# Weight words without GpSimd, a deferred sigmoid and separate summary products in a fused attention and channel-mix kernel

## The chip, the cores and the metric

The kernel runs on one NeuronCore of a Trainium2 chip. The metric is the device time of one execution in microseconds (us). The core has five instruction streams: PE (TensorE, matrix products), DVE (VectorE), ACT (ScalarE), POOL (GpSimd) and SP (which here only issues DMA transfers). Each works through its own queue strictly in order and waits on semaphores for the others. PE has a second row in the profile, PEld, for the loads of its stationary operand.

## The reference

Two stages, one after the other. The first is attention over 4 batches, 8 heads, 768 tokens and 64 features. A query sees the keys less than 16 positions away, and besides these 24 summary keys (the maximum over each block of 32 keys) with summary values (the mean over the block):

```python
k_sum = k.reshape(B, H, nb, block, D).max(axis=3)
v_sum = v.reshape(B, H, nb, block, D).mean(axis=3)
scores_l = where(|i - j| < 16, scale * q @ k.T, -1e9)
scores_s = scale * q @ k_sum.T + log(32)
a = softmax over [scores_l, scores_s]
x = a @ [v, v_sum]                     # heads side by side: 512 features
```

The second is a channel mix on these 512 features, with each token and the one before it (`xp`):

```python
xk = mu_k * x + (1 - mu_k) * xp
xr = mu_r * x + (1 - mu_r) * xp
k  = relu(xk @ w_k) ** 2               # 512 -> 1024
v  = k @ w_v                           # 1024 -> 512
out = sigmoid(xr @ w_r) * v
```

The three weight matrices come as 64-bit floats. The kernel gets them as pairs of 32-bit words and makes the fp32 values itself.

## The kernel before, in words

**Units.** Attention is cut into 32 units: a batch, a pair of heads, a half of the 768 tokens (384, six windows of 64 queries). For one unit PE makes the scores (L480), DVE adds the mask and finds the maximum (L491), ACT takes the exponentials and their sums (L495), DVE the reciprocals (L502), POOL multiplies by them in six instructions (L506, "the norms"), PE transposes (L513), ACT copies the result out of PSUM (L517), and PE multiplies by the values (L535). In each window 96 rows are local keys and 24 are summaries. In batch 0 the block means come from PE (L416, L436), and DVE or POOL copies them six times side by side into the 24 summary rows of each value tile (L444). In the later batches a DMA does that.

**Channel mix.** For each half batch ("token tile" of 384) the shift and mix is made per pair of heads: ACT or POOL multiplies by `1 - mu` (L560 or L563), DVE adds `mu * x` (L566), ACT rounds to fp32r (L569) and DVE takes the rest (L571). With these high and low parts PE makes the gate (`w_r`, L612 to L614), whose sigmoid ACT takes (L628). Then for j = 0 to 7 the experts: twelve products with block j of `w_k` (L644), relu and square on ACT (L649, L651), a rounded part (L653 on DVE or L654 on ACT) and a rest (L655), and nine products with block j of `w_v` (L666, the last block L692), which accumulate in three PSUM banks. L698 multiplies by the gate, and a DMA stores.

PSUM has four banks named `mm`. While the experts run, three of them hold the accumulators. The fourth is passed between the products with `w_k` and the gate of the second half of batch 0, which is made in three pieces between blocks 5, 6 and 7 of the first half: the next product can start only when ACT has read the bank.

**Weights.** 20 blocks of 128 x 512 values (four `w_r`, eight `w_k`, eight `w_v`) are made while batch 0 runs. For one block: a DMA into a buffer `st` (three of them), a scaling of the high word on ACT (L323) or POOL (L326), the sign on POOL (L331, high word times zero), two instructions on DVE that shift and join the bits (L335, L339), the rounding to fp32r on ACT (L347) or POOL (L349), and the rest on DVE (L361). Buffers: two `we` for sign and low bits, two `wc` for the words that are being made.

**Order.** All of this is recorded as operations with due times. A planner then simulates the engines with a table of lengths and puts the operations in order on each engine; where an operation has two ways (ACT or POOL, DVE or ACT) it also chooses the engine. `NUDGE` shifts single due times. Warm-up products (L727) fill PE where it waits during the first 33 us. The order is fixed in the program: an engine doesn't pass over an instruction that waits.

## Time and profile before

| | |
|---|---|
| three timed runs | 471.42, 472.8, 473.5 us; median 472.8 us |
| the profiled execution | 474.23 us, of which 472.4 us lie between its first and last instruction (the span) |
| PE busy | 442.6 us, 94% of the span |
| PEld busy | 374.6 us, 79% |
| ACT busy | 293.4 us, 62% |
| DVE busy | 272.5 us, 58% |
| POOL busy | 145.6 us, 31% |
| DMA | 51.18 MB |

The shares are averages over stages that differ much. From some 120 us on PE is busy without a gap nearly to the end. Before that, with batch 0 and the weights, DVE and POOL are the fullest. So a row here is read by window of time. PE's busy time is modelled at its ends and hides small gaps; the loads (PEld) are a second measure of how dense PE's work is.

### The profile page before, as it was taken

To read this page: it belongs to the slowest core of one execution; us is meant where nothing else is said; L and a number is where in the kernel's file an instruction comes from. 1 tells how busy PE (TensorE), PEld (TensorE's weight loads), DVE (VectorE), ACT (ScalarE), POOL (GpSimd) and SP (SyncE) were. 2 spreads that over 40 slices of the span, in tenths; PEclk is the share of its full clock that TensorE was granted. 3 is DMA by queue.
4 is the path that set the end of the run, shared out by engine and by line. 5 is a ranking of instruction groups with operands and counts; after the bars stand their busy time and mean duration, and the time that the engine had idled before them with its cause. 6 is when DMAs were issued, how large, how long until landed. Compare 5 with 4: busy or idle time off the path is not lost.

```text
span 472.4 us, 9665 instructions
## 1 busy us (share of the span) xinstructions
PE 442.6 (94%) x3531; PEld 374.6 (79%) x3531; DVE 272.5 (58%) x825; ACT 293.4 (62%) x842; POOL 145.6 (31%) x281
## 2 busy tenths in 40 slices
PE   1698699799999999999999999999999999999996
PEld 0586486687888878997888888997888888888995
DVE  4679997999646376537355467438455455223223
ACT  2767886769788686528895756429886655232311
POOL 0469898642413131302352202303252201000000
PEclk9999989799999999999999999999999999999999
DMA  8994446777410036944100307905100010001001
GB/s 270 288 272 127 137 139 212 221 235 216 138 40 15 20 122 171 242 119 150 46 23 8 111 35 230 280 5 176 47 14 12 5 68 1 1 0 68 0 2 67
DMA packets 27159, 51.18 MB, mean 108 GB/s; under 512 B 2919, under 2 KB 15079, under 8 KB 27111
## 3 DMA queue, kind: packets, MB, share of 16 engines
q1 hardware_dynamic: 27111, 50.56, 35.8%
q8 instruction: 28, 0.46, 0.4%
q14 instruction: 20, 0.16, 0.1%
HBM read 42.49 MB, written 6.29 MB: 103 GB/s over the span
## 4 chain that ended last, share of the span: by engine, by line
PE 81%; POOL 8%; DMA 3%; ACT 2%; DVE 2%; issue 1%; SPq 1%; DVEq 0%; POOLq 0%
PE mm L644 26%; PE mm L666 24%; PE av L535 4%; PE sc L480 4%; POOL y L506 4%; PE mm L612 4%; PE mm L614 4%; PE mm L613 4%; PE pt L513 4%; PE mm L692 3%; DMA mask_sb<-in_mask 2%; DMA st<-in_w_v 1%; POOL we L331 1%; ACT y L495 1%; PE av L727 1%
## 5 line engine op out<-in xcount | busy, mean ns | idle before, releaser
L506 POOL TENSOR_SCALAR y<-y,rc 128x120 f32<-128x120 f32 x192 | 87.8, 476 | 118.6 <-DVE rc L502 114.6
L644 PE MATMUL mm<-xs,wk_h 128*128 128x384 f32 x512 | 104.3, 346 | 5.2 <-ACT r L649 3.4
L644 PEld LDWEIGHTS mm<-xs,wk_h 128*128 128x128 f32 x512 | 91.7, 192 | 9.7 <-ACT r L649 3.8
L649 ACT ACTIVATE r<-mm 128x384 f32<-128x384 f32 x64 | 31.3, 489 | 91.0 <-PE mm L644 90.6
L495 ACT ACTIVATE y<-y,mn 128x120 f32<-128x120 f32 x192 | 73.7, 387 | 5.7 <-DVE mn L491 5.5
L666 PE MATMUL mm<-wv_h,kh 128*128 128x512 f32 x168 | 68.8, 409 | 0.1
L666 PE MATMUL mm<-wv_l,kh 128*128 128x512 f32 x168 | 66.8, 398 | 0.5 <-DVE wv_l L361 0.5
L491 DVE CUSTOM_DVE_ANT_0 y<-sc,mask_sb 128x120 f32<-128x120 f32 x192 | 42.7, 275 | 24.8 <-PE sc L480 15.2
L644 PE MATMUL mm<-xs,wk_l 128*128 128x384 f32 x256 | 55.8, 340 | 0.0
L571 DVE TENSOR_TENSOR xs<-xa,xs 128x384 fp32r<-128x384 f32 x64 | 37.6, 592 | 30.0 <-ACT xs L569 29.7
L653 DVE CAST kh<-r 128x384 fp32r<-128x384 f32 x38 | 14.1, 372 | 63.5 <-ACT r L651 63.0
L666 PE MATMUL mm<-wv_h,kl 128*128 128x512 f32 x168 | 50.0, 406 | 0.0
L644 PEld LDWEIGHTS mm<-xs,wk_l 128*128 128x128 f32 x256 | 46.2, 190 | 0.0
L655 DVE TENSOR_TENSOR kl<-r,kh 128x384 fp32r<-128x384 f32 x64 | 38.1, 595 | 14.0 <-ACT kh L654 7.7
L566 DVE SCALAR_TENSOR_TENSOR xa<-vx,mu_sb,xa 128x384 f32<-128x384 f32 x64 | 42.3, 677 | 5.6 <-POOL xa L563 2.8
L563 POOL TENSOR_SCALAR xa<-vx,om_sb 128x384 f32<-128x384 f32 x23 | 18.3, 796 | 82.5 <-DVE xs L571 55.2
L480 PE MATMUL sc<-kt,qt 64*64 64x120 f32 x768 | 29.2, 280 | 14.6 <-DMA qt<-in_q 8.3
L517 ACT COPY pts<-pt 120x384 f32<-120x384 f32 x64 | 30.4, 475 | 15.6 <-PE pt L513 15.0
L612 PE MATMUL mm<-wr_h,xs 128*128 128x512 f32 x96 | 39.0, 406 | 0.0
L480 PEld LDWEIGHTS sc<-kt,qt 64*64 64x64 f32 x768 | 21.1, 138 | 22.3 <-DVE kt L404 8.3
L513 PE MATMUL pt<-ident_sb,y 128*120 128x128 f32 x192 | 34.7, 285 | 4.0 <-POOL y L506 3.7
L614 PE MATMUL mm<-wr_h,xs 128*128 128x512 f32 x96 | 38.0, 395 | 0.0
(71 smaller groups left out, 728.1 us busy)
## 6 DMA issues: line engine op xcount, KB each, us to landing
vx<-in_v SPq DMA_DIRECT2D x32, 360.0 KB
kt<-in_k SPq DMA_DIRECT2D x15, 544.0 KB
qt<-in_q SPq DMA_DIRECT2D x32, 192.0 KB
out<-z SPq DMA_DIRECT2D x23, 256.0 KB
st<-in_vT SPq DMA_DIRECT2D x12, 384.0 KB
st<-in_w_k SPq DMA_DIRECT2D x8, 512.0 KB
st<-in_w_v SPq DMA_DIRECT2D x8, 512.0 KB
st<-in_w_r SPq DMA_DIRECT2D x4, 512.0 KB
```

Of the source, the lines that this page charges most:

```text
L480: nc.tensor.matmul(sc[h].t[cs, i, 0:NK], qt.t[hs, n * QW:(n + 1) * QW], kt.t[hs, w * KB:w * KB + NK], start=True, stop=True,)
L491: op("DVE", "mask", None, lambda h=h, i=i, var=var: nc.vector.tensor_tensor_reduce(out=y[h].t[:, i, :], in0=sc[h].t[:, i, 0:NK], in1=mask_ ...
L495: op("ACT", "exp", None, lambda h=h, i=i: nc.scalar.activation(y[h].t[:, i, :], y[h].t[:, i, :], AF.Exp, bias=mn[h].t[:, i:i + 1], scale=-1.0,
L506: op("POOL", "norm", None, lambda h=h, i=i: nc.gpsimd.tensor_scalar(out=y[h].t[:, i, :], in0=y[h].t[:, i, :], scalar1=rc.t[:, NSL * h + i: ...
L513: nc.tensor.transpose(out=pt[h].t[0:NK, i * P:(i + 1) * P], in_=y[h].t[:, i, :], identity=ident_sb)
L566: op("DVE", "mixd", None, lambda xt=xt, xa=xa, p=p: nc.vector.scalar_tensor_tensor(out=xa.t, in0=xt.t[:, 1 + lo:1 + lo + HT], scalar=mu_sb ...
L571: op("DVE", "sub", None, lambda xa=xa, xh=xh, xl=xl: nc.vector.tensor_tensor(out=xl.t, in0=xa.t, in1=xh.t.bitcast(F32), op=ALU.subtract), ...
L612: nc.tensor.matmul(ps[i].t, xh.t[:, ts], wr_h[:, p, :], start=(p == 0), stop=False)
L614: nc.tensor.matmul(ps[i].t, xl.t[:, ts], wr_h[:, p, :], start=False, stop=(p == NPAIR - 1))
L644: nc.tensor.matmul(ps.t[:, 0:HT], w[:, j, p, :], x[p][s].t, start=(n == 0), stop=(n == 11))
L655: op("DVE", "sub", None, lambda: nc.vector.tensor_tensor(out=kl.t, in0=r.t, in1=kh.t.bitcast(F32), op=ALU.subtract), reads=[(r, 0), (kh, 0 ...
L666: nc.tensor.matmul(acc[t].t, a.t[:, t * P:(t + 1) * P], w[:, j, :], start=start, stop=stop)
```

## The change

- The sign of a weight block is no longer made on POOL. DVE shifts the low word (a new instruction, L323 of the new program), then takes the sign bit from the high word and joins it (L326), then joins with the scaled word as before (L330): three instructions instead of two.
- Scaling and rounding of weight blocks are ACT's alone; POOL has no choice there any more. In batch 0 the multiplication by `1 - mu` is ACT's alone too.
- `st` has four buffers instead of three, `we` one instead of two.
- The gate of the second half of batch 0 is copied out of PSUM (L618) and its three sigmoids are taken together later (L748).
- In batch 0 the summary values are not copied into the value tiles. Each unit has two products of its own, one per head, of the 24 summary rows with all 384 queries, ahead of the products of its six windows. The 24 rows in the value tiles are zero there.
- An unused constant (`minus_sb`) is gone. The planner's lengths and nudges are other numbers.

```diff
-    e003=-1000, e004=8000, e005=3000, e013=-40000, e016=-20000, e017=-3000, f000=-8000,
+    e003=-3000, e011=-21000, e012=3000, e016=-2000, e017=-3000, f003=3000, f006=-10000,
...
-APART = False
+APART = True
...
-        st=tiles("st", 3, [P, 1024], U32), we=tiles("we", 2, [P, 512], U32), wc=tiles("wc", 2, [P, 512], U32),
+        st=tiles("st", 4, [P, 1024], U32), we=tiles("we", 1, [P, 512], U32), wc=tiles("wc", 2, [P, 512], U32),
...
+        def low():
+            nc.vector.tensor_scalar(out=we.t, in0=words()[1], scalar1=29, scalar2=None, op0=ALU.logical_shift_right)
 
         def sign():
-            nc.gpsimd.tensor_scalar(
-                out=we.t.bitcast(F32), in0=words()[0].bitcast(F32), scalar1=0.0, scalar2=1.0, op0=ALU.mult, op1=ALU.mult)
-
-        def low():
             nc.vector.scalar_tensor_tensor(
-                out=we.t, in0=words()[1], scalar=29, in1=we.t, op0=ALU.logical_shift_right, op1=ALU.bitwise_or)
+                out=we.t, in0=words()[0], scalar=0x80000000, in1=we.t, op0=ALU.bitwise_and, op1=ALU.bitwise_or)
...
-        op("ACT", "wscale", None, scale_act, reads=[(st, 0)], writes=whole, other=("POOL", "wscale_p", scale_pool))
-        op("POOL", "wsign", None, sign, reads=[(st, 0)], writes=[(we, 0)])
-        op("DVE", "wor", None, low, reads=[(st, 0), (we, 0)], writes=[(we, 0)])
+        op("ACT", "wscale", None, scale_act, reads=[(st, 0)], writes=whole)
+        op("DVE", "wbits", None, low, reads=[(st, 0)], writes=[(we, 0)])
+        op("DVE", "wor", None, sign, reads=[(st, 0), (we, 0)], writes=[(we, 0)])
...
-           reads=whole, writes=[((name, i), "h")],
-           other=("POOL", "wcast_p", lambda: nc.gpsimd.tensor_scalar(
-               out=dst_h, in0=wc.t.bitcast(F32), scalar1=1.0, scalar2=1.0, op0=ALU.mult, op1=ALU.mult)))
+           reads=whole, writes=[((name, i), "h")])
...
-                        start=not own, stop=True,
+                        start=not own, stop=not own or w == HW - 1,
...
-               other=("POOL", "mixa_p", lambda xt=xt, xa=xa, p=p: nc.gpsimd.tensor_scalar(
+               other=None if b == 0 else ("POOL", "mixa_p", lambda xt=xt, xa=xa, p=p: nc.gpsimd.tensor_scalar(
...
+            if later:
+
+                op("ACT", "zcopy", None, lambda i=i, t=t: nc.scalar.copy(out=z[t].t, in_=ps[i].t),
+                   reads=[(ps[i], 0)], writes=[(z[t], 0)],
+                   other=("DVE", "zcopy_d", lambda i=i, t=t: nc.vector.tensor_copy(out=z[t].t, in_=ps[i].t)))
+                continue
...
+        if n == 1:
+            z = tokens[1][1]
+            plan.tag = "gate01s"
+            op("ACT", "sigmoid3", e2_due(0, 1, 4), lambda: [nc.scalar.activation(a.t, a.t, AF.Sigmoid) for a in z],
+               reads=[(a, 0) for a in z], writes=[(a, 0) for a in z])
```

What it does to the order is seen at three places. The first is POOL's queue before, from the sign of weight block `wv1` to the rounding of `wk2` (`we`, `wc`: weight words; `y`: a unit's probabilities; `xa`: a mix):

```order
L331 TENSOR_SCALAR we_140<-st_137 128x512
L506 TENSOR_SCALAR y_89<-y_89,rc_101 128x120 x3
L506 TENSOR_SCALAR y_90<-y_90,rc_101 128x120 x3
L331 TENSOR_SCALAR we_139<-st_138 128x512
L349 TENSOR_SCALAR wk_h<-wc_141 128x512
L326 TENSOR_SCALAR wc_142<-st_137 128x512
L506 TENSOR_SCALAR y_91<-y_91,rc_102 128x120 x3
L506 TENSOR_SCALAR y_92<-y_92,rc_102 128x120 x3
L563 TENSOR_SCALAR xa_113<-vx_76,om_sb 128x384
L326 TENSOR_SCALAR wc_141<-st_138 128x512
L349 TENSOR_SCALAR wk_h<-wc_141 128x512
```

And POOL's queue after, from the same unit's norms on:

```order
L495 TENSOR_SCALAR y_89<-y_89,rc_101 128x120 x3
L495 TENSOR_SCALAR y_90<-y_90,rc_101 128x120 x3
L495 TENSOR_SCALAR y_91<-y_91,rc_102 128x120 x3
L495 TENSOR_SCALAR y_92<-y_92,rc_102 128x120 x3
L393 COPY kt_61<-ks_80 128x12x24
L495 TENSOR_SCALAR y_89<-y_89,rc_100 128x120 x3
L495 TENSOR_SCALAR y_90<-y_90,rc_100 128x120 x3
```

Signs, scalings, roundings and mixes have left the places between the norms. The second place is DVE's queue where the late weight blocks are made. Before (L335 and L339 join the bits, L361 is the rest, L566 and L571 belong to a mix, L655 to an expert):

```order
L339 SCALAR_TENSOR_TENSOR wc_142<-wc_142,we_140 128x512
L339 SCALAR_TENSOR_TENSOR wc_141<-wc_141,we_139 128x512
L655 TENSOR_TENSOR kl_135<-r_131,kh_133 128x384
L571 TENSOR_TENSOR xs_121<-xa_113,xs_120 128x384
L335 SCALAR_TENSOR_TENSOR we_140<-st_136,we_140 128x512
L361 TENSOR_TENSOR wk_l<-wc_141,wk_h 128x512
L361 TENSOR_TENSOR wv_l<-wc_142,wv_h 128x512
L335 SCALAR_TENSOR_TENSOR we_139<-st_137,we_139 128x512
L339 SCALAR_TENSOR_TENSOR wc_141<-wc_141,we_140 128x512
```

After (L323 is the new shift; L326 and L330 stand for L335 and L339, L350 for L361, L555 for L566, L560 for L571):

```order
L323 TENSOR_SCALAR we_140<-st_137 128x512
L350 TENSOR_TENSOR wk_l<-wc_142,wk_h 128x512
L560 TENSOR_TENSOR xs_117<-xa_111,xs_116 128x384
L326 SCALAR_TENSOR_TENSOR we_140<-st_137,we_140 128x512
L555 SCALAR_TENSOR_TENSOR xa_113<-vx_70,mu_sb,xa_113 128x384
L330 SCALAR_TENSOR_TENSOR wc_141<-wc_141,we_140 128x512
L560 TENSOR_TENSOR xs_119<-xa_112,xs_118 128x384
L323 TENSOR_SCALAR we_140<-st_138 128x512
L560 TENSOR_TENSOR xs_121<-xa_113,xs_120 128x384
L326 SCALAR_TENSOR_TENSOR we_140<-st_138,we_140 128x512
L350 TENSOR_TENSOR wv_l<-wc_141,wv_h 128x512
L330 SCALAR_TENSOR_TENSOR wc_142<-wc_142,we_140 128x512
```

Each block has one instruction more here, and with one `we` buffer the blocks follow one another strictly. The third place is ACT's queue around the last piece of the second gate (`z`: a gate; `mm_147`: the fourth bank; L649 reads the next product's bank). Before:

```order
L569 CAST xs_118<-xa_113 128x384
L628 ACT_TABLE_LOAD
L628 ACTIVATE z_110<-mm_147 128x512
L517 COPY pts_104<-pt_145 120x384
L569 CAST xs_120<-xa_111 128x384
L495 ACT_TABLE_LOAD
L495 ACTIVATE y_89,sm_98<-y_89,mn_93 128x120 x2
L649 ACTIVATE r_131<-mm_147 128x384
```

After (L618 is the copy, L644 stands for L649, L338 for L347):

```order
L649 CAST kh_132<-r_130 128x384
L558 CAST xs_114<-xa_111 128x384
L618 COPY z_110<-mm_147 128x512
L558 CAST xs_116<-xa_112 128x384
L338 CAST wv_h<-wc_141 128x512
L549 ACTIVATE xa_111<-vx_70,om_sb 128x384
```

The loads of the activation table stand no longer ahead of the reading of the bank; the rounding of the last weight block now stands behind it.

More of the change, by code (lines that the diff above doesn't have):

```diff
@@ L41 @@
     e2a=1400, e2b=700, e2=700, e2h=350, resulth=400, e2_32=2800, e2l_32=930,
-    warm=220, kred=860, kred2=470, kmax=190, kcopy=340, vred=860, mask=204, rc=190, evac=475, mixd=620, sub=490, khv=340,
-    result=695, wsign=720, eps=190, wor=740, wsub=625, tiny=60,
-    exp=380, pts=400, vm=160, mixa=540, cast=440, relu=525, square=530, sigmoid=500, wscale=570, wcast=530,
+    warm=220, kred=860, kred2=470, kmax=190, kcopy=340, vred=860, mask=204, rc=190, evac=475, mixd=570, sub=490, khv=340,
+    result=695, wbits=360, eps=190, zcopy=540, zcopy_d=610, sigmoid3=1500, wor=650, wsub=630, tiny=60,
+    exp=380, pts=400, vm=160, mixa=540, cast=440, relu=525, square=530, sigmoid=500, wscale=590, wcast=545,
     norm=470, wscale_p=640, wcast_p=640, mixa_p=860, kcopy_p=630, evac_a=375, fill=735,
@@ L61 @@
 NUDGE = dict(
-    e003=-1000, e004=8000, e005=3000, e013=-40000, e016=-20000, e017=-3000, f000=-8000,
-    f001=3000, f002=3000, f003=-1000, f005=1000, f006=25000, f007=9000, f010=25000,
-    f011=8000, f013=3000, f014=-20000, f015=3000, f017=25000, gate01=-3000, gate10=-8000,
-    mix010=-8000, set12=7000, set13=3000, unit001=-3000, unit020=1000, unit100=1000, unit101=16000,
-    unit110=8000, unit111=-9000, unit120=-39000, unit130=8000, unit131=11000, wk1=3000, wk3=20000,
-    wk4=3000, wk6=4000, wk7=-20000, wr0=-21000, wr3=8000, wv3=7000, wv4=3000,
-    wv5=-1000, wv6=-8000, wv7=-19000,
+    e003=-3000, e011=-21000, e012=3000, e016=-2000, e017=-3000, f003=3000, f006=-10000,
+    f007=20000, f011=1000, f012=8000, f013=17000, f014=6000, f015=3000, f016=-8000,
+    gate01s=7000, mix010=-20000, set00=1000, set10=-2000, set11=-8000, set12=-5000, set13=-8000,
+    unit000=-20000, unit020=-1000, unit030=3000, unit101=-1000, unit110=-4000, unit111=11000, unit120=8000,
+    unit121=-20000, unit130=3000, wk3=3000, wk4=1000, wk7=-20000, wr0=3000, wv0=5000,
+    wv1=-1000, wv4=8000, wv5=7000,
 )
@@ L197, in schedule @@
                 o.cost *= 1.6
-            if o.name in ("exp", "sigmoid"):
-                if table not in (None, o.name):
+            if o.name in ("exp", "sigmoid", "sigmoid3"):
+                if table not in (None, o.name[:7]):
                     start += TABLE
-                table = o.name
+                table = o.name[:7]
             o.start = start
@@ L281, in tile_kernel @@
         out=om_sb, in0=mu_sb, scalar1=-1.0, scalar2=1.0, op0=ALU.mult, op1=ALU.add), reads=MU, writes=OM)
-    minus_sb = const.tile([P, P], F32R, name="minus_sb")
-    op("ACT", "vm", None, lambda: nc.scalar.activation(minus_sb, ident_sb, AF.Copy, scale=-1.0), reads=IDENT, writes=[("minus", 0)])
     kinds = sorted({w for _, _, w in MIX_PE}, reverse=True)
@@ L602, in mixed, with gate @@
         return (mixes_pe if (b, hf, which) in MIX_PE else mixes)(b, hf, which)
-    def gate(b, hf, x, z, tiles, by_pair=False):
+    def gate(b, hf, x, z, tiles, by_pair=False, later=False):
         plan.tag = f"gate{b}{hf}"
@@ L748, in tile_kernel @@
             tokens[1] = mixed(0, 1, 1), [buf("z") for _ in range(NTT)]
-            between = {j: [lambda t=t: gate(0, 1, *tokens[1], [t])] for t, j in enumerate(BETWEEN)}
+            between = {j: [lambda t=t: gate(0, 1, *tokens[1], [t], later=True)] for t, j in enumerate(BETWEEN)}
+        if n == 1:
[3 more added lines that the diff above has]
+               reads=[(a, 0) for a in z], writes=[(a, 0) for a in z])
         experts(b, hf, x, tokens[n][1], between)
```

3 lines of the change are left out of this document (removed).

## The prediction

> **What bounds the kernel now.** I read the busy time by window first. The cuts are points where PE stands or starts a new phase; the columns are PE, PEld, DVE, ACT and POOL busy time, the granted PE clock, and DMA.
>
> ```profile
> core 0: us, PE busy (x) PEld busy (x) DVE busy (x) ACT busy (x) POOL busy (x), PEclk, DMA share, GB/s
> 26.00:60.32 34.32, 28.57 (x357) 21.35 (x347) 31.86 (x100) 27.61 (x91) 27.77 (x39) 0.98 0.53 166
> 60.32:87.70 27.38, 22.79 (x188) 18.73 (x188) 24.02 (x49) 19.62 (x57) 24.32 (x32) 0.94 0.56 173
> 87.70:121.40 33.70, 31.99 (x203) 26.49 (x203) 32.42 (x87) 27.21 (x64) 14.62 (x25) 0.92 0.77 229
> 121.40:185.00 63.60, 63.60 (x586) 54.40 (x586) 35.01 (x116) 47.33 (x149) 17.26 (x44) 1.00 0.30 86
> 185.00:472.40 287.40, 283.60 (x2050) 243.75 (x2048) 135.96 (x428) 159.30 (x446) 52.84 (x122) 1.00 0.24 71
> ```
>
> From 121.4 us PE never stands, and its loads fill 86% of the time (54.40 of 63.60). The change leaves that stretch's products alone. Everything at stake lies before. In the first three windows PE stands 5.75 + 4.59 + 1.71 = 12.1 us, and a lower clock costs some 0.02 x 34 + 0.06 x 27 + 0.08 x 34 = 5.0 us: 17 us are the most that can go. By PEld the first two windows are emptier than that (62% and 68% against 86%), so PE has room there for more products. The fullest engines are DVE (93, 88, 96%) and POOL (81, 89%); ACT has 34.32 + 27.38 - 47.23 = 14.5 us free before 87.7 us.
>
> The chain of waits, taken between 38 and 81 us, says which of them is decisive; then PE's own rows in order of time, and ACT's around two of them (the idle time before each, and who ended it, in brackets):
>
> ```profile
> by line: POOL y L506 48.1%; POOL we L331 12.4%; POOL wc L326 8.6%; issue 6.2%; POOL xa L563 5.6%; POOL wk_h L349 4.4%; POOL wv_h L349 3.7%; POOL vx L444 2.7%; DVE we L335 2.5%; DVE xa L566 2.3%; POOL wr_h L349 2.2%; DVE wc L339 1.4%; ACT pt
> ```
> ```profile
> 59.22 0.81 PE L513 MATMUL pt<-ident_sb,y 128*120 128x128 f32 x2 [1.40 <-POOL y L506]
> ...
> 87.70 2.93 PE L644 MATMUL mm<-xs,wk_h 128*128 128x384 f32 x8 [3.44 <-ACT r L649]
> ...
> 119.06 1.66 PE L644 MATMUL mm<-xs,wk_h 128*128 128x384 f32 x8 [1.71 <-ACT z L628]
> ```
> ```profile
> 83.14 0.69 ACT L323 ACTIVATE wc<-st 128x512 f32<-128x512 f32 x1 [2.12 <-DVE wk_l L361]
> ...
> 117.12 1.28 ACT L628 ACT_TABLE_LOAD   x1
> 118.42 0.60 ACT L628 ACTIVATE z<-mm 128x512 f32<-128x512 f32 x1
> ```
>
> So from 38 to 81 us the chain lies on POOL's queue, half of it norms that stand between wide weight work. DVE is 90% full beside it and so next in line. At 87.7 us PE waited for a relu that stood on ACT behind a scaling, which had waited 2.12 us for DVE. At 119.06 it waited for a sigmoid behind a table load.
>
> **The change part by part.** *POOL's wide work goes.* What that frees is DVE's time too: the same DVE instructions run longer while POOL is full. DVE's groups in 0 to 25 us (POOL mostly idle), then in 36 to 106 us, then in 190 to 400 us:
>
> ```profile
> L339 DVE SCALAR_TENSOR_TENSOR wc<-wc,we 128x512 uint32<-128x512 uint32 x3 | 2.1, 689 | 0.2
> L335 DVE SCALAR_TENSOR_TENSOR we<-st,we 128x512 uint32<-128x512 uint32 x3 | 2.0, 681 | 5.0 <-POOL vx L545 5.0
> ...
> L361 DVE TENSOR_TENSOR wr_l<-wc,wr_h 128x512 fp32r<-128x512 f32 x2 | 1.4, 688 | 0.3 <-ACT wr_h L347 0.3
> ```
> ```profile
> L335 DVE SCALAR_TENSOR_TENSOR we<-st,we 128x512 uint32<-128x512 uint32 x17 | 14.1, 830 | 2.2 <-POOL we L331 2.2
> L339 DVE SCALAR_TENSOR_TENSOR wc<-wc,we 128x512 uint32<-128x512 uint32 x17 | 13.0, 780 | 0.2
> L566 DVE SCALAR_TENSOR_TENSOR xa<-vx,mu_sb,xa 128x384 f32<-128x384 f32 x10 | 8.2, 830 | 0.7 <-POOL xa L563 0.7
> L571 DVE TENSOR_TENSOR xs<-xa,xs 128x384 fp32r<-128x384 f32 x10 | 7.4, 736 | 0.0
> L361 DVE TENSOR_TENSOR wk_l<-wc,wk_h 128x512 fp32r<-128x512 f32 x8 | 6.5, 809 | 0.0
> L361 DVE TENSOR_TENSOR wv_l<-wc,wv_h 128x512 fp32r<-128x512 f32 x7 | 6.1, 875 | 1.1 <-POOL wv_h L349 1.1
> ...
> L655 DVE TENSOR_TENSOR kl<-r,kh 128x384 fp32r<-128x384 f32 x6 | 4.6, 771 | 0.0
> ```
> ```profile
> L566 DVE SCALAR_TENSOR_TENSOR xa<-vx,mu_sb,xa 128x384 f32<-128x384 f32 x34 | 21.5, 646 | 3.7 <-POOL xa L563 2.1 <-ACT xa L560 1.4
> ...
> L571 DVE TENSOR_TENSOR xs<-xa,xs 128x384 fp32r<-128x384 f32 x33 | 18.7, 568 | 22.2 <-ACT xs L569 22.2
> L655 DVE TENSOR_TENSOR kl<-r,kh 128x384 fp32r<-128x384 f32 x32 | 18.5, 579 | 8.7 <-ACT kh L654 7.4 <-PE mm L666 0.4
> ...
> L653 DVE CAST kh<-r 128x384 fp32r<-128x384 f32 x20 | 7.2, 362 | 16.3 <-ACT r L651 16.1
> ```
>
> The stretch is 17 x 0.149 + 17 x 0.091 + 8 x 0.121 + 7 x 0.187 + 10 x 0.184 + 10 x 0.168 + 6 x 0.192 = 11.0 us. POOL's groups in the same 70 us:
>
> ```profile
> L506 POOL TENSOR_SCALAR y<-y,rc 128x120 f32<-128x120 f32 x30 | 21.1, 721 | 0.1
> L331 POOL TENSOR_SCALAR we<-st 128x512 f32<-128x512 f32 x17 | 14.4, 852 | 3.3 <-DVE wc L339 2.4 <-DMA st<-in_w_k 0.9
> L326 POOL TENSOR_SCALAR wc<-st 128x512 f32<-128x512 f32 x9 | 8.6, 956 | 3.5 <-DVE wk_l L361 2.3 <-DVE wv_l L361 1.2
> L563 POOL TENSOR_SCALAR xa<-vx,om_sb 128x384 f32<-128x384 f32 x4 | 3.8, 958 | 1.3 <-DVE xs L571 1.3
> L349 POOL TENSOR_SCALAR wk_h<-wc 128x512 fp32r<-128x512 f32 x4 | 3.5, 866 | 1.1 <-DVE wc L339 1.1
> ```
>
> The norms stay, 21.1 us; 30.3 us of these rows go, 59%. I give the stretch back in that proportion, 6.5 us, of which 51.7/70 lies before 87.7 us: -4.8 us. Bounds: 0 if the norms alone cause it, -8.1 if the wide work does. DVE's waits for POOL in these rows, 2.2 + 1.1 + 0.7 = 4.0 us, go too.
>
> *DVE gets the shift.* No row shows a one-input instruction on every second word. Nearest are the cast, 0.362 us for 384 values, and the spreading copy in 26 to 60 us:
>
> ```profile
> L444 DVE COPY vx<-vm 24x768 f32<-24x768 f32 x3 | 1.8, 613 | 0.4 <-ACT vm L438 0.3
> ```
>
> Between them 512 values take 0.45 us; the dear end is L335's 0.68 for the strided read. I take 0.45, since it too has one input. In the new order 11 shifts stand behind 26 us and before block `wk4`, where PE's 87.7 us stands now: +5.0 us (up to 7.5). The Trainium skill prices it lower: "VectorE: DVE Perf Modes", section "Mode 2×_2P — use both read ports for one tensor", lets a one-source instruction in SBUF do two elements per cycle and names no condition on the stride; from its cycle table I estimate 0.33 us, and the sum would be 1.3 us lower. No run here shows it yet.
>
> *Spreads go*: three after 26 us, 3 x 0.613 = -1.8 us. *Two expert casts* come over from ACT before that point, +0.7; a reduction, a copy and small maxima come ahead, two joins and a subtraction go behind: about +0.5 by their durations. DVE's balance up to 87.7 us: -4.8 - 4.0 - 1.8 + 5.0 + 0.7 + 0.5 = -4.4 us.
>
> *ACT gets what POOL loses.* Its prices, from 26 to 121.4 us:
>
> ```profile
> L560 ACT ACTIVATE xa<-vx,om_sb 128x384 f32<-128x384 f32 x12 | 7.4, 614 | 0.4 <-DVE xs L571 0.4
> L323 ACT ACTIVATE wc<-st 128x512 f32<-128x512 f32 x8 | 5.5, 686 | 5.3 <-DVE wk_l L361 2.5 <-DMA kt<-in_k 1.5 <-DVE wv_l L361 1.1
> ...
> L347 ACT CAST wk_h<-wc 128x512 fp32r<-128x512 f32 x4 | 2.5, 619 | 1.7 <-DVE wc L339 1.7
> ```
>
> Before block `wk4` the two orders differ by seven scalings, six roundings and three mixes more on ACT, less some copies and casts: 4.8 + 3.7 + 1.8 - 2.5 = 7.8 us. They go into its 14.5 us of free time, so in the sum they cost no work; but ACT and DVE are then both over 90% full, in order, and each rounding stands between two DVE instructions. I put new waits of DVE for ACT at +2.0 us, half of what it lost to POOL (bounds: none, or all 7.8 if ACT's free time can't be used). Up to 87.7 us: **-2.4 us**.
>
> *Deferred sigmoid.* PE's 1.71 us at 119 us go: the copy stands on ACT without a table load ahead. If instead the bank waits behind the scalings of `wv7`, two or three instructions of 0.6 to 0.7 us bring it all back. I take **-1.7**. The lower clock from 87.7 to 121.4 us cost 0.08 x 33.7 = 2.7 us, after a stand of 3.44 us; I take half, **-1.4**, since that stand shrinks but doesn't vanish.
>
> *Summary products.* Two products of 384 columns are 4 instructions x 384 = 1536 columns, as many as a unit's 24 of 64:
>
> ```profile
> 23.31 0.92 PE L535 MATMUL av<-pts,vx 120*64 120x64 f32 x24
> ...
> 28.50 1.28 PE L727 MATMUL av<-ident_sb 128*128 128x128 f32 x10
> ```
>
> So 0.92 us a unit, if the two heads run side by side as they do there; one after the other, by the warm-up's 0.128 us per 128 columns, 1.54 us. Eight units make 7.4 (12.3) us of PE time. Five stand before PE's first expert product, two up to 87.7 us, one behind, hidden by the standing PE has there (by PEld against 86%: 34.32 - 21.35 / 0.86 and 27.38 - 18.73 / 0.86, 15.1 us); five warm-ups fewer pay back 1.3. What the new order puts behind 121.4 us (a score, two transposes) was in the third window before, so it cancels there. More `st` buffers only let weights land earlier: no term.
>
> Sum: -2.4 - 1.7 - 1.4 = -5.5 us. The profiled execution (474.2 us, span 472.4 and 1.8 around it) becomes 468.7 us. The median of the runs shown is 1.4 us below that execution, so I predict **467.3 us** for a median.
>
> **The rivals** (times as medians). *The norms alone stretch DVE.* Then -4.8 doesn't come: 467.3 + 4.8 = 472.1 us, no change. For it: norms average 0.721 us in the window, so they too wait for DVE; against: most of POOL's time was wide work. The Trainium skill speaks for it: "SBUF — State Buffer", section "Who interferes with whom", has a DVE instruction with two SBUF inputs and a GpSimd instruction that reads SBUF lock each other out whole, and norms are of that kind; the stretched rows all have two inputs, which agrees.
>
> *ACT becomes the queue that all wait for* (the slower side). Place: ACT between 26 us and `wk4`, scalings and roundings among exponentials. If its 14.5 us of waiting stay, because they come from DVE and PE, its 47.2 + 7.8 us need 69.5 us instead of 61.7: +7.8, and with -3.1 from the later terms the end is 472.8 + 4.7 = 477.5 us. It decides once more than 9.8 of the 14.5 us stay. For it: the 2.12 us at 83.14; against: the free time is nearly twice what is added.
>
> *Everything closes up.* Full clock, no new waits for ACT, stretch back to the bound: -4.4 - 3.3 - 1.7 - 2.7 = -12.1, 460.7 us. For it: the 12.1 + 5.0 us at stake; against: two engines over 90%.
>
> *The shift is dear*, 0.68 us: 11 x 0.23 = +2.5, 469.8 us.
>
> **How the numbers follow.** Chances: forecast 0.45, norms 0.17, ACT 0.16, all closed up 0.14, dear shift 0.08. Runs of this kernel can't be told apart below about 0.5%, 2.4 us. Faster by more: 0.45 + 0.14 and most of the dear shift, 0.65; same 0.19; slower 0.16. The forecast's own range is 464 to 470.4; the range to hold 8 times in 10 reaches to the closed-up case and nearly to ACT's: 460 to 476.
>
> **What would show it.** POOL's norms nearer 0.45 than 0.721 us, and POOL out of the chain between 38 and 81 us. L330 and L350 near 0.69, the shift near 0.45. The product that now starts at 87.70 starts near 85, the one at 119.06 near 113, and no wait there for ACT `z`. From there the rest is as long as now, 353 us to the end of the span. I am wrong if DVE's two-input rows stay at 0.78 to 0.87, or if DVE's waits for ACT before 87 us exceed some 6 us, or if PE stands at the summary products.

## The result and the profile after

| | before | changed | ratio, 95% interval |
|---|---|---|---|
| first comparison, medians of 4 runs each | 472.19 us | 466.19 us | 0.9864 [0.9842, 0.9886] |
| on another chip, 11 and 5 runs | 471.81 us | 464.99 us | 0.985 [0.9823, 0.9877] |

Predicted were 467.3 us. The profiled execution of the changed kernel took 467.03 us, its span is 465.2 us. Its busy time by window, cut where the same products start as in the rows of before (columns as there):

```profile
26.00:61.62 35.62, 33.55 (x410) 23.69 (x408) 29.13 (x105) 30.31 (x95) 15.14 (x26) 0.95 0.63 194
61.62:86.45 24.83, 24.83 (x232) 20.14 (x230) 22.99 (x60) 23.92 (x65) 9.64 (x16) 1.00 0.81 253
86.45:110.50 24.05, 23.23 (x128) 19.15 (x127) 23.80 (x62) 19.07 (x47) 4.43 (x6) 1.00 0.65 195
110.50:185.00 74.50, 74.50 (x683) 63.76 (x682) 48.55 (x175) 57.46 (x180) 22.49 (x52) 1.00 0.35 101
```

The first expert product starts at 61.62 us, that of block 4 at 86.45, that of block 7 at 110.50. Between them PE stands only 0.8 us, at full clock. From 26 us to 61.62 it stands 2.1 us and has a stretch at low clock (granted clock 0.95 in the mean of that window). The chain of waits between 38 and 81 us:

```profile
by line: DMA qt<-in_q 11.7%; POOL y L495 10.1%; PE mm L639 9.2%; PE mm L601 8.8%; PE mm L602 7.7%; PE mm L603 7.4%; PE sc L469 5.6%; ACT y L484 4.9%; issue 4.6%; DVE wc L330 4.6%; PE av L524 3.9%; PE av L517 3.7%; PE pt L502 3.5%; DVE we L3
```

POOL's queue is no longer that chain; PE's own products are its largest part. DVE's and POOL's groups from 36 to 106 us:

```profile
L326 DVE SCALAR_TENSOR_TENSOR we<-st,we 128x512 uint32<-128x512 uint32 x15 | 10.4, 694 | 0.1
L330 DVE SCALAR_TENSOR_TENSOR wc<-wc,we 128x512 uint32<-128x512 uint32 x15 | 10.3, 687 | 1.3 <-ACT wc L320 1.2
L555 DVE SCALAR_TENSOR_TENSOR xa<-vx,mu_sb,xa 128x384 f32<-128x384 f32 x14 | 8.8, 643 | 1.7 <-ACT xa L549 1.7
...
L323 DVE TENSOR_SCALAR we<-st 128x512 uint32<-128x512 uint32 x16 | 7.0, 437 | 0.1
L560 DVE TENSOR_TENSOR xs<-xa,xs 128x384 fp32r<-128x384 f32 x11 | 6.2, 567 | 0.2 <-ACT xs L558 0.2
L350 DVE TENSOR_TENSOR wk_l<-wc,wk_h 128x512 fp32r<-128x512 f32 x7 | 4.9, 700 | 0.2 <-ACT wk_h L338 0.2
```
```profile
L495 POOL TENSOR_SCALAR y<-y,rc 128x120 f32<-128x120 f32 x32 | 22.3, 713 | 39.1 <-DVE rc L491 38.0 <-ACT pts L506 1.1
```

The two-input rows of DVE are back at what they take alone. The norms on POOL are as slow as before.

### The profile page after: what moved, and what is told of

The parts are those of the page before. It is cut to its first block, busy times and chain, and to the rows that moved or that the text cites. A ratio compares the mean times of both kernels' runs of the same rounds, so it can differ in the third digit from the quotient of the medians.

```text
span 465.2 us, 9712 instructions
## 1 busy us (share of the span) xinstructions
PE 442.9 (95%) x3553; PEld 372.5 (80%) x3553; DVE 268.0 (58%) x856; ACT 297.8 (64%) x853; POOL 106.7 (23%) x233
## 4 chain that ended last, share of the span: by engine, by line
PE 87%; DMA 5%; DVE 3%; ACT 2%; POOL 1%; issue 1%; SPq 0%; DVEq 0%
PE mm L639 27%; PE mm L661 24%; PE mm L601 5%; PE av L524 5%; PE mm L602 5%; PE mm L603 5%; PE pt L502 5%; PE sc L469 5%; PE mm L687 3%; DMA pool_sb<-in_pool 2%; PE av L722 1%; DMA st<-in_w_r 1%; DMA qt<-in_q 1%; POOL y L495 1%; PE mm L405 1%
## 5 line engine op out<-in xcount | busy, mean ns | idle before, releaser
L495 POOL TENSOR_SCALAR y<-y,rc 128x120 f32<-128x120 f32 x192 | 89.5, 486 | 157.7 <-DVE rc L491 152.8
L639 PE MATMUL mm<-xs,wk_h 128*128 128x384 f32 x512 | 101.3, 340 | 0.0
L639 PEld LDWEIGHTS mm<-xs,wk_h 128*128 128x128 f32 x512 | 90.1, 188 | 4.8 <-issue 0.8
L644 ACT ACTIVATE r<-mm 128x384 f32<-128x384 f32 x64 | 31.3, 489 | 89.4 <-PE mm L639 89.4
L648 DVE CAST kh<-r 128x384 fp32r<-128x384 f32 x51 | 18.5, 363 | 70.4 <-ACT r L646 67.3
L560 DVE TENSOR_TENSOR xs<-xa,xs 128x384 fp32r<-128x384 f32 x64 | 35.7, 557 | 31.7 <-ACT xs L558 31.6
L555 DVE SCALAR_TENSOR_TENSOR xa<-vx,mu_sb,xa 128x384 f32<-128x384 f32 x64 | 39.8, 636 | 8.8 <-ACT xa L549 7.9
L650 DVE TENSOR_TENSOR kl<-r,kh 128x384 fp32r<-128x384 f32 x64 | 36.4, 568 | 10.6 <-PE mm L661 4.5
L602 PE MATMUL mm<-wr_l,xs 128*128 128x512 f32 x96 | 38.6, 402 | 0.0
L661 PEld LDWEIGHTS mm<-wv_h,kh 128*128 128x128 f32 x168 | 31.6, 188 | 6.5 <-issue 0.5
L484 ACT ACTIVATION_READ_ACCUMULATOR y<-y,mn 128x1 f32 x192 | 36.5, 190 | 0.0
```

The lines of the kernel that those rows point to most:

```text
L484: op("ACT", "exp", None, lambda h=h, i=i: nc.scalar.activation(y[h].t[:, i, :], y[h].t[:, i, :], AF.Exp, bias=mn[h].t[:, i:i + 1], scale=-1.0,
L495: op("POOL", "norm", None, lambda h=h, i=i: nc.gpsimd.tensor_scalar(out=y[h].t[:, i, :], in0=y[h].t[:, i, :], scalar1=rc.t[:, NSL * h + i: ...
L555: op("DVE", "mixd", None, lambda xt=xt, xa=xa, p=p: nc.vector.scalar_tensor_tensor(out=xa.t, in0=xt.t[:, 1 + lo:1 + lo + HT], scalar=mu_sb ...
L560: op("DVE", "sub", None, lambda xa=xa, xh=xh, xl=xl: nc.vector.tensor_tensor(out=xl.t, in0=xa.t, in1=xh.t.bitcast(F32), op=ALU.subtract), ...
L602: nc.tensor.matmul(ps[i].t, xh.t[:, ts], wr_l[:, p, :], start=False, stop=False)
L639: nc.tensor.matmul(ps.t[:, 0:HT], w[:, j, p, :], x[p][s].t, start=(n == 0), stop=(n == 11))
```

## The experiments

"Block 0" below is the first expert product, "block 4" and "block 7" the first product with those blocks of `w_k`. "The changed kernel" is its second profiled execution, of the first run below.

**Both kernels again.**

> The changed kernel as it is, for comparison on the same chip: 466.2 us, ratio 0.986. Product that starts e003 -> e004 (the one at 87.70 us before) again near 86.5 us, the one at 119.06 before again near 110.5.

> The kernel before as it is, a second profiled execution. The first one (span 472.4 us, mean clock 0.989) was longer than the median and had two stretches of half clock, near 59 to 63 and 86 to 93 us. Theory A (the 27.4 us from the first expert product to the product of block 4, and the 31.4 from there to block 7, belong to the program): both come again within 0.5 us. Rival B (1 to 3 us of them were a lower clock that this execution happened to have): with another clock 25.5 to 26.5 and 28.5 to 30.5 us.

| profiled execution | block 0 at | block 0 to 4 | block 4 to 7 | block 7 to PE's end |
|---|---|---|---|---|
| before | 60.32 | 27.38 | 31.37 | 349.6 |
| before, second | 58.77 | 27.41 | 31.30 | 349.7 |
| changed | 61.62 | 24.83 | 24.05 | 351.0 |
| changed, second | 59.80 | 24.82 | 24.18 | 351.1 |

From block 0 on both programs repeat to 0.15 us, the low clock of the kernel before behind block 4 included; theory A holds. (The low clock near 60 us in the first execution of before did not come again; block 0 to 4 is as long without it.) Only the start differs, by 1.5 to 1.8 us from one execution to another. So the change costs 1.0 to 1.3 us before block 0, gains 2.6 and 7.2 us in the next two stretches, and gives 1.4 us back behind them: 7.2 us in all.

The loss before block 0 lies in the start. In the new order the load of the pooling matrix is issued later, at 8.2 us against 6.0 in the second executions, and PE waits for it. Its first pooling product there, before and after:

```profile
15.35 1.51 PE L416 MATMUL mm<-vx,pool_sb 120*32 120x128 f32 x24
```
```profile
17.39 1.51 PE L405 MATMUL mm<-vx,pool_sb 120*32 120x128 f32 x24 [2.31 <-DMA pool_sb<-in_pool]
```

From that product to block 0 the changed kernel takes 42.4 us and the kernel before 43.4 (42.5 and 43.5 in the first executions). So the change gains 1.0 us there, and a start that is 2.0 to 2.3 us later takes it away.

The two stretches behind block 0 in the second execution of before, by window:

```profile
58.77:86.18 27.41, 22.69 (x187) 17.57 (x188) 24.03 (x51) 19.55 (x57) 24.35 (x32) 0.97 0.54 176
86.18:117.48 31.30, 29.59 (x188) 24.33 (x188) 31.12 (x83) 24.96 (x61) 12.44 (x19) 0.91 0.78 239
```

What PE waited for between 26 us and block 7, in the second execution of before and of the changed kernel (us in total, times, longest):

```profile
PE pt L513 <- POOL y L506: 3.8, 5, 1.4
PE mm L644 <- ACT r L649: 3.4, 1, 3.4
PE av L535 <- ACT pts L517: 1.8, 4, 0.7
PE mm L644 <- ACT z L628: 1.7, 1, 1.7
PE sc L480 <- DVE mn L491: 0.6, 3, 0.2
PE mm L666 <- DVE wv_l L361: 0.5, 1, 0.5
```
```profile
PE pt L502 <- POOL y L495: 1.0, 2, 0.7
PE pt L502 <- ACT sm L489: 0.9, 1, 0.9
PE mm L601 <- ACT r L644: 0.8, 2, 0.6
```

Of some 12 us of waits 2.7 are left. Work has moved too: between block 0 and 4 PE now has 232 instructions instead of 187, between 4 and 7 128 instead of 188. So the 7.2 us gained between block 4 and 7 hold work that went into the stretch ahead and, as the 1.4 us show, behind block 7.

**The value loads earlier.**

```diff
+    late = [o for o in order if o.eng == "SP" and o.tag == "set02"][0]
+    move = [o for o in order if o.eng == "SP" and o.tag == "set00"][2:4] + [plan.ops[2]]
+    order = [o for o in order if o not in move]
+    at = order.index(late)
+    order[at:at] = move
```

> The changed program with three loads moved ahead on SP: the two loads of batch 0's values and the load of the pooling matrix (pool_sb) come before the keys of the third unit set. In the trace of the changed kernel the first pooling product waits 3.62 us for pool_sb and starts at 19.11 us; before the change it started at 16.80. Theory A (this late start is what brings the first expert product 1.3 us later than before): pooling starts near 17, the first expert product (L634's first, now at 61.6 us) comes 1.5 to 2.3 us earlier, total 464.2 us. Rival B (the time up to there is set by DVE's and PE's amount of work, a later wait takes over): the first pooling product is earlier, the expert product moves by less than 0.5 us, total 466 us.

Measured: 468.54 us, 3.6 us slower than the changed kernel beside it; ratio to before 0.992 [0.9894, 0.9946]. Neither theory was tested: the load of the pooling matrix was issued 1.5 us earlier (6.65 us), but the first pooling product started at 17.38 us, and so it did in the changed kernel this time (17.39): of the 19.11 in its first execution, 1.7 us were that execution's. Block 0 came at 62.71 us, 45.3 us behind the pooling product instead of 42.4, with the keys of the third set behind the moved loads. So the order of the first loads matters, and this one is worse; what an earlier pooling product would be worth in the new order stays open.

**The sigmoids at their old place.**

```diff
-  lambda i=i, t=t: nc.scalar.copy(out=z[t].t, in_=ps[i].t)
+  lambda i=i, t=t: nc.scalar.activation(z[t].t, ps[i].t, AF.Sigmoid)
-  lambda: [nc.scalar.activation(a.t, a.t, AF.Sigmoid) for a in z]
+  lambda: None
```

> The changed program, but the three pieces of the second gate leave PSUM by a sigmoid again instead of by a copy, in the same places of ACT's queue, and the joint sigmoids later are left out: one edit of the change undone, order kept. Theory A (the sum's term): only the last piece is waited for, by a table load of 1.28 us and a sigmoid: the product of block 7 comes 1.5 to 2 us later than 110.5, total +1.7, 467.9 us. Rival B (ACT has no slack before the product with block 4 to 7 any more): three pieces with two table loads each delay weights too, product of block 7 at 113 or later, total 469 us or more. Rival C (ACT's free time takes it): no change of the total.

Measured: 468.34 us, 3.4 us more than 464.99; ratio 0.9914 [0.9882, 0.9946]. Block 4 to 7 takes 25.90 us instead of 24.18, 1.7 us more as in theory A, and from block 7 to the next product PE loses as much again. ACT's rows there, and PE's:

```profile
106.91 1.28 ACT L618 ACT_TABLE_LOAD   x1
108.20 0.60 ACT L618 ACTIVATE z<-mm 128x512 f32<-128x512 f32 x1
...
110.66 1.28 ACT L484 ACT_TABLE_LOAD   x1
...
113.89 0.46 ACT L506 COPY pts<-pt 120x384 f32<-120x384 f32 x1
```
```profile
95.57 0.50 PE L601 MATMUL mm<-wr_h,xs 128*128 128x512 f32 x1 [1.55 <-ACT r L644]
...
104.48 0.50 PE L601 MATMUL mm<-wr_h,xs 128*128 128x512 f32 x1 [0.45 <-ACT r L644]
...
114.50 0.52 PE L502 MATMUL pt<-ident_sb,y 128*120 128x128 f32 x3 [1.62 <-ACT pts L506]
```

The size of theory A comes, its mechanism doesn't: the product of block 7 waits for no sigmoid. PE waits for relus instead, which stand on ACT behind the pairs of loads of the earlier pieces: 1.55 us, 0.58 in the changed kernel, and 0.45, none there. The way back to the exponential's table costs a second load, and behind the last one stands a copy of transposes, for which PE waits 1.62 us.

**DVE without the shift.**

```diff
-            nc.vector.tensor_scalar(out=we.t, in0=words()[1], scalar1=29, scalar2=None, op0=ALU.logical_shift_right)
+            pass
-   in1=we.t, op0=ALU.bitwise_and, op1=ALU.bitwise_or)
+   in1=words()[0], op0=ALU.bitwise_and, op1=ALU.bitwise_and)
```

> The changed program without the shift: 20 instructions of 0.437 us less on DVE, some 11 of them between 26 us and the product of block 4. The three low bits of every weight are left out of the computation. It asks what DVE's time is worth now. Theory A (DVE still sets the pace up to block 4, so a microsecond of DVE is a microsecond of time): the product of block 4 comes 3.5 to 5 us earlier than 86.5, total 462 us. Rival B (with POOL's wide work gone and DVE's two-input instructions at 0.69, the chain lies elsewhere, on PE's and ACT's waits): block 4 moves by 1 us or less, total 465.5 us or more.

Measured: 467.3 us, ratio 0.9894 [0.9864, 0.9924]; not faster, rather 2 us slower, with a mean granted clock of 0.989 to 0.999 in these runs against 0.996 in all of the changed kernel's. Its profiled execution has a span of 463.5 us against 463.6; block 0 to 4 takes 25.88 us and 4 to 7 24.06. Its first pooling product started 1.15 us later, and from there block 0 comes 2.1 us earlier; PE kept its full clock on the way. So 8.7 us less work on DVE bring, counted from there, 1.2 us up to block 7 in this execution and nothing in the median: theory A falls. DVE's amount of work is no longer the bound from block 0 on. Why the median is higher stays open.

**The sign on POOL again.**

```diff
-            nc.vector.tensor_scalar(out=we.t, in0=words()[1], scalar1=29, ...)
+            nc.gpsimd.tensor_scalar(out=we.t.bitcast(F32), in0=words()[0].bitcast(F32), scalar1=0.0, ...)
...
-   out=we.t, in0=words()[0], scalar=0x80000000, in1=we.t, op0=ALU.bitwise_and, ...
+   out=we.t, in0=words()[1], scalar=29, in1=we.t, op0=ALU.logical_shift_right, ...
```

> The changed program with one part undone, order kept: the sign is made on POOL again (20 instructions of 512 elements at the places where the shift stands on DVE), and DVE joins with two instructions instead of three. DVE has 20 x 0.437 us less to do. Theory A (POOL's wide instructions lengthen DVE's two-input ones, and DVE waits for POOL): rows of L326, L330 and L350 back from 0.69 to 0.75 or more, DVE waits for POOL again, block 0 to block 4 takes 25.5 to 27 us instead of 24.8, total 466.5 to 468 us against the changed kernel's 465.0. Rival B (what counts is DVE's amount of work): faster by 1 us or more. Rival C (neither lies on the chain of waits now): 465 us within 0.7, although the rows stretch.

Measured: 468.39 us, ratio 0.9903 [0.9869, 0.9937]. Against 0.985 this is 0.5%, 2.5 us; the two intervals overlap. Block 0 to 4 takes 25.14 us, 4 to 7 25.09. DVE's groups from 36 to 106 us, and its waits from 26 to 87 us:

```profile
L327 DVE SCALAR_TENSOR_TENSOR we<-st,we 128x512 uint32<-128x512 uint32 x15 | 10.6, 709 | 6.5 <-POOL we L323 6.5
L331 DVE SCALAR_TENSOR_TENSOR wc<-wc,we 128x512 uint32<-128x512 uint32 x15 | 10.3, 686 | 1.4 <-ACT wc L320 1.3
```
```profile
DVE we L327 <- POOL we L323: 6.4, 7, 1.5
```

The time is near theory A's, the reason only half: with one `we` buffer and in this order DVE mostly waits while POOL makes the sign, so its rows hardly stretch (0.709 and 0.686 us). What is left as the cause is the wait. What the sign costs with two `we` buffers no run shows.

**Idle work on POOL, in wide and in narrow pieces.**

```diff
     for o in order:
         o.emit()
+        if o.name == "wbits":
+            for _ in range(2):
+                nc.gpsimd.tensor_scalar(
+                    out=junk[:, 0:360], in0=mask_sb.rearrange("p a b -> p (a b)")[:, 0:360], scalar1=0.5, scalar2=1.0, op0=ALU.mult, op1=ALU.mult)
```

The narrow run has `range(6)` and 120 instead of 360.

> The changed program with 40 idle instructions of 128 x 360 elements added on POOL, two at each weight block, which nobody waits for. In the two traces a two-input DVE instruction that begins while POOL runs one of 512 elements takes up to 0.47 us longer, one of 384 elements up to 0.33, one of 120 elements (a norm) up to 0.11. Theory A (DVE is kept out only while POOL streams its elements in, about 0.9 ns each): those that are hit take up to 0.33 us longer, the means of L326, L330, L350, L555 and L560 rise by 0.05 to 0.2 us. Rival B (each keeps the other out for the whole instruction): up to 0.5 us and more longer, means up by over 0.25. The time: +1 to +3 us if DVE still sets the pace, nothing if PE does, apart from what the norms behind the added instructions are late.

> The changed program with 120 idle instructions of 128 x 120 elements added on POOL, six at each weight block: as many elements as in the run with 40 wide ones, in pieces as long as a norm. Theory A (DVE is kept out for a POOL instruction's elements only): two-input DVE rows rise by 0.1 us at most, no single one by more than some 0.12, while the norms and the added instructions take 0.6 to 0.7 us beside DVE instead of 0.37. Rival B (whole instructions are locked): DVE rows rise by as much as with the wide ones or more. The time: norms are late behind up to six added instructions, so it may be longer than with the wide ones although DVE is freer; if DVE's rows decide, it is the shorter of the two.

Measured: wide 473.67 us, 1.0016 [0.9983, 1.005]; narrow 474.9 us, 1.003 [0.9998, 1.0063]. Either takes the whole gain back, more than was expected. Where POOL runs wide pieces without a gap, from 84 to 92 us, DVE's groups are these; below, the changed kernel's at the same place of the program, 82.5 to 90 us:

```profile
L560 DVE TENSOR_TENSOR xs<-xa,xs 128x384 fp32r<-128x384 f32 x3 | 2.5, 833 | 0.0
L330 DVE SCALAR_TENSOR_TENSOR wc<-wc,we 128x512 uint32<-128x512 uint32 x2 | 1.9, 965 | 0.0
L326 DVE SCALAR_TENSOR_TENSOR we<-st,we 128x512 uint32<-128x512 uint32 x1 | 1.0, 971 | 0.0
```
```profile
L560 DVE TENSOR_TENSOR xs<-xa,xs 128x384 fp32r<-128x384 f32 x4 | 2.2, 553 | 0.0
L330 DVE SCALAR_TENSOR_TENSOR wc<-wc,we 128x512 uint32<-128x512 uint32 x2 | 1.4, 688 | 0.0
L326 DVE SCALAR_TENSOR_TENSOR we<-st,we 128x512 uint32<-128x512 uint32 x2 | 1.4, 686 | 0.0
```

Each is 0.28 us longer, whatever its own length, while the POOL pieces take 0.49 to 0.97 us. Over 26 to 125 us, the 24 two-input instructions that begin while a piece of 360 runs are longer by 0.22 us in the mean and 0.29 at most, against what the same instruction takes with POOL idle; those that begin beside pieces of 120 (83 in the narrow run) by 0.04 and 0.17, and 0.11 but for the one that met three pieces; beside those of 512 in the kernel before (26) by 0.39 and 0.47. So theory A on the mechanism: DVE is held for POOL's elements, by the largest cases 0.8 to 0.9 ns each, not for POOL's whole instruction. Summed over these windows the stretch is some 6 us in the wide run and 3.5 in the narrow one, 1 in the changed kernel and 13 in the kernel before. In the wide run it sits on the path: DVE is full from block 4 on (28.45 of 28.97 us), ACT's scalings and roundings wait for it, and PE stands 2.67 us for a relu behind them and runs at low clock afterwards. From the pooling product to block 0 this run takes 2.0 us more than the changed kernel, from block 4 to 7 4.8 us more. In the narrow run it is the norms behind the added pieces:

```profile
57.41 1.15 PE L502 MATMUL pt<-ident_sb,y 128*120 128x128 f32 x3 [3.90 <-POOL y L495]
```

**Without the summary products.**

```diff
-            if own:
+            if False:
...
-                        start=not own, stop=not own or w == HW - 1,
+                        start=True, stop=True,
```

> The changed program without the two summary products of each unit of batch 0 (32 matrix instructions of 24 x 384 in all); the summaries' share of batch 0's output is left out of the computation. In the changed kernel such a pair of products takes 0.79 us from start to start. Theory A (the prediction's: they lie in time in which PE would stand anyway): at most 1 us, total 465 us. Rival B (PE is the bound from the first expert product on, and close to it before): the two pairs between block 0 and block 4 come off in full, 24.8 - 1.6 = 23.2 us, and up to four of the five before it come off the first expert product's start; total 460 to 463.5 us.

Measured: 464.03 us, ratio 0.9809 [0.9782, 0.9836], 0.4% or 1.9 us less than the changed kernel by the ratios, whose intervals overlap a little. Block 0 comes at 56.76 us, 3.0 us earlier, of which 0.9 us are the start; from the first pooling product it is 2.1 us. Block 0 to 4 takes 23.83 us, 1.0 less, where both programs repeat to 0.15 us. Block 4 to 7 takes 1.1 more, where a wait opens:

```profile
85.03 0.50 PE L601 MATMUL mm<-wr_h,xs 128*128 128x512 f32 x1 [1.40 <-ACT r L644]
```

So the products are on the path, nearer to rival B than to theory A. But not in full: three pairs (not two) lie between block 0 and 4, 2.4 us by their starts, of which 1.0 comes off, the wait behind block 4 takes that back, and the total lies above rival B's 463.5.

**Norms on DVE.**

```diff
-  op("POOL", "norm", None, lambda h=h, i=i: nc.gpsimd.tensor_scalar(
+  op("POOL", "norm", None, lambda h=h, i=i, on=nc.vector if plan.tag in ON_DVE else nc.gpsimd: on.tensor_scalar(
...
+    for tag in ON_DVE:
+        norms = [o for o in order if o.name == "norm" and o.tag == tag]
+        order = [o for o in order if o not in norms]
+        at = 1 + [(o.name, o.tag) for o in order].index(("rc", tag))
+        order[at:at] = norms
```

> The changed program with the 12 norms of two units (the two whose norms begin at 49.6 and 55.1 us in the second profiled execution of the changed kernel) on DVE, directly behind their reciprocals, instead of on POOL. There each six take 4.33 and 4.01 us on POOL beside DVE's two-input instructions, against 2.2 us when they run alone; PE waits 0.70 + 0.31 us for them and runs at half clock from 54.0 to 57.4 us behind that. Theory A (those norms are the chain up to the first expert product, and DVE has time to spare, as the run without the shift says): the transposes behind them come 2 us or more earlier, PE keeps its clock, the first expert product comes 1.5 to 4 us earlier, total 461.5 to 463.5 us against 465.0. Rival B (a later wait, for DVE's mixes or ACT, takes over): less than 0.7 us. Rival C (DVE is pushed back by the 12 instructions and its mixes come later): slower.

Measured: 468.01 us, ratio 0.9892 [0.9869, 0.9916], by the ratios 2 us slower than the changed kernel, with intervals that overlap. Six norms take 1.24 us on DVE, but the transposes behind them wait again:

```profile
51.22 0.54 PE L503 MATMUL pt<-ident_sb,y 128*120 128x128 f32 x3
53.60 0.90 PE L503 MATMUL pt<-ident_sb,y 128*120 128x128 f32 x3 [1.84 <-ACT pts L507]
```

The copy `pts` stands on ACT behind three mixes, which wait for DVE, now later. PE then runs at low clock to block 0, at 61.91 us, 44.4 us behind the pooling product instead of 42.4. Rivals B and C together: POOL's norms were only one of three queues that meet at this place.

**The kernel before with its stand filled.**

```diff
     for o in order:
+        if (o.name, o.tag) == ("e1", "e004"):
+            for _ in range(12):
+                nc.tensor.matmul(spare, ident_sb, ident_sb, start=True, stop=True)
         o.emit()
```

> The kernel before with 12 warm-up products (24 matrix instructions of 0.128 us, 3.1 us) put on PE directly ahead of the product of block 4, where PE stands for 3.4 us and behind which its products take twice as long, from 87.7 to 93.3 us in the first profiled execution. The time up to there stays as it is. Theory A (the low clock is the price of that stand, in each execution): the products behind run at full clock, block 4 to block 7 takes 2.3 to 2.8 us less than 31.4, total 469 to 470 us against 471.8 to 472.8 before; this is what the clock term of the prediction should have been, 2.7 and not 1.4. Rival B (ACT's and DVE's work is the bound right behind block 4, so a faster PE only waits): block 4 to 7 shorter by less than 1 us. Rival C (the low clock comes for another reason): it stays.

Measured: 471.78 us beside 472.69, ratio 0.9994 [0.997, 1.0019]: no difference that these runs can tell. The profile shows why. In the second execution of before, and here:

```profile
86.18 2.93 PE L644 MATMUL mm<-xs,wk_h 128*128 128x384 f32 x8 [3.42 <-ACT r L649]
```
```profile
83.18 2.95 PE L761 MATMUL av<-ident_sb 128*128 128x128 f32 x24 [0.74 <-ACT vx L549]
85.88 1.68 PE L644 MATMUL mm<-xs,wk_h 128*128 128x384 f32 x8
```

The eight products take 1.68 us instead of 2.93, and the granted clock is 1.00 over all of block 4 to 7 instead of 0.91: the stand causes the low clock. But block 4 to 7 gets only 0.7 us shorter (30.59 against 31.30): rival B. In the kernel before a faster PE waits there: its standing from block 4 to 7 grows from 1.71 to 2.43 us.

**Copies instead of summary products, and a filled stand.**

```diff
-            if own:
+            if False:
...
+    for on, tag, hf in halves:
+        vm, vw = sums[tag]
+        on.tensor_copy(
+            out=windows(vw[hf])[QW:KB], in_=vm.t[QW:KB].unsqueeze(1).broadcast_to([NS, HW, P]))
...
+    for _ in range(fill[i]):
+        nc.tensor.matmul(spare, ident_sb, ident_sb, start=True, stop=True)
```

> The changed program with two edits, which the profile tells apart. First, one part of the change undone, the rest of the order kept: the summary values are copied into the value tiles again (four copies of about 0.61 us on DVE for the first half of batch 0, four of about 1.16 us on POOL for the second), and the units' own summary products are left out. Second, six warm-up products (12 matrix instructions, 1.5 us) stand between the transposes at 50.6 to 54.0 us of the changed kernel, where PE waits 0.70 + 0.94 + 0.31 us and runs at half clock behind them. Theory A (PE is the bound from 17 us on, so the summary products are on the path and copies are the cheaper way; the half clock comes from those waits): the first expert product starts 2.5 to 3 us earlier than 59.8, as without the products, and 1.5 us more by the clock, the first nine gate products behind the transposes take 0.23 us each instead of 0.43, total 461 to 463 us against the changed kernel's 465.0 to 466.2 and against 464.0 without the products. Rival B (DVE and POOL are late by the copies): the first expert product no earlier, total 465 us or more. Rival C (a wait behind block 4 takes it back, as in the run without the products, where block 4 to 7 took 1.1 us longer): 463.5 to 464.5 us.

Measured: 469.69 us, ratio 0.9935 [0.9914, 0.9957], rival B. POOL's last copy waited 6.34 us for the summaries and held the norms behind it, and PE stood for them:

```profile
41.71 1.21 POOL L768 COPY vx<-vm 24x768 f32<-24x768 f32 x1 [6.34 <-ACT vm L427]
43.02 4.30 POOL L496 TENSOR_SCALAR y<-y,rc 128x120 f32<-128x120 f32 x6
```

The filled stand did what it should: the nine gate products behind it run at full clock (PEclk 1.00 from 50 to 60 us, 0.83 in the changed kernel's slice there). But the low clock came at 46 to 50 us instead, behind the new stand. What copies in better places would cost stays open. Of the runs that leave nothing of the computation out, none was faster than the changed kernel.

## Why the prediction was right, and where not

The time came within 1.1 us, in part by luck: the terms missed on both sides and cancelled. Up to block 4 the profiled executions gained 1.3 to 1.6 us where 2.4 were forecast, from there to block 7 7.2 where 3.1 were, and behind it they lost 1.4 where nothing was.

- **DVE's stretch and its waits for POOL** (-4.8 and -4.0): the mechanism held, the size of the first was too small. The rows are back at 0.69, 0.64 and 0.57 us, the whole 11.0 us, not 59%. The step that failed is the share: it took norms and wide work as equal per microsecond, while a norm holds DVE for its 120 elements and a wide one for 512. The rival that the norms alone stretch DVE is out, and "norms nearer 0.45" was wrong as well: at 0.713 us they are the ones that wait. The Trainium skill, which spoke for that rival ("SBUF — State Buffer", "Who interferes with whom"), calls the port pair that both engines share "an exclusive lock". That agrees with the norms' side: in the changed kernel's second execution five of six norms (49.6 to 53.9 us) end 0.16 to 0.24 us behind the end of a two-input DVE instruction. On DVE's side the runs show holds shorter than POOL's instructions, 0.28 us beside pieces of 0.49 to 0.97.
- **The shift**, 0.45 us: 0.437 measured. The Trainium skill's two elements per cycle ("VectorE: DVE Perf Modes", "Mode 2×_2P — use both read ports for one tensor", estimated at 0.33) do not come out for this operation.
- **New waits for ACT**, +2.0: DVE's waits for ACT from 26 to 87 us rose from 2.0 to 6.3 us in the first two executions and from 0.3 to 6.9 in the second two, over the bound of 6 that was to prove me wrong; the largest of them in the changed one:

```profile
DVE xa L555 <- ACT xa L549: 4.2, 3, 2.5
...
DVE wc L330 <- ACT wc L320: 1.2, 1, 1.2
```

  The time didn't follow, and the run without the shift shows why: from block 0 on DVE's amount of work moves nothing any more. That test was put on an engine that the change takes off the path.
- **Up to block 4**, -2.4 in sum: 87.70 to 86.45 us, and 86.18 to 84.62 in the second pair, -1.3 to -1.6. The sum has no term for the order of the first loads, and so none for the pooling product that starts 2.0 to 2.3 us later; counted from that product, block 4 comes 3.6 us earlier in both pairs. Between block 0 and 4 PE is busy throughout in the changed kernel (24.83 of 24.83 us, 20.14 of loads): DVE's balance of -4.4 could not be cashed beyond that. I took DVE to stay the bound; from block 0 on PE had become it.
- **Summary products**, 0: this step failed. "Hidden by the standing PE has there" used the standing of the kernel before, which the same change removes. They cost some 1.9 us in the time, and in the profiled executions 2.1 us between the first pooling product and block 0 and 1.0 behind it. With the later start, that is why block 0 comes no earlier. A pair takes 0.79 us from start to start (0.92 was taken), so the unit price was near; three pairs, not two, stand between block 0 and 4.
- **The deferred sigmoid**, -1.7: mis-sized, 3.4 us measured, with the sigmoids put back into the new order. I counted one wait, for the last piece. In the new order no product waits for a piece: half of the 3.4 us are relus behind the loads of the earlier pieces, the other half is a copy of transposes behind the load on the way back, which I forgot.
- **The clock**, -1.4: right by accident. The low clock from block 4 to 7, 0.09 x 31.3 = 2.8 us, is gone altogether, where I took half. But filling the stand alone was worth 0.7 us, because PE then waits. It pays off only with the waits gone, and so is no term that could be added by itself. A stretch of low clock lies ahead of block 0: nine gate products take 3.8 us there in the changed kernel's second execution, and 2.3 at full clock in the one without the shift.
- **What was put behind**, 0: 1.4 us more from block 7 to the end, by the instruction counts out of the stretch ahead. The 353 us to the end of the span became 354.7. That cancels, as forecast, against a gain ahead that was larger than forecast.

From block 0 to 7 it is the rival in which everything closes up: 58.7 to 49.0 us, with waits of 6.4 us down to 0.8 and no low clock. Against it stand the late start, the products at the start and the work put behind.

Not tested by themselves are the numbers of `st` and `we` buffers, the planner's lengths and nudges, and the new order that follows from them all. The single effects measured (3.4 us for the sigmoids, 2.5 for the sign, 1.9 lost on the summary products) were each taken inside the new order and need not add up to the 7 us.

## What to carry to other kernels

Ask of a cost that is called hidden whether the change itself removes its cover: the stands of the kernel before were the cover for the summary products, and the same edit filled them. Keep wide work off POOL while DVE's two-input instructions are on the path, and price what POOL does to DVE by its elements, not by its time. When one engine has become dense, time saved on another can be worth nothing, as the run without the shift shows, while time added to it can still cost all, as the idle work on POOL does.
